# A gated attention and token-mixing block: first x block and wq loaded by columns, q ahead of k and v, and a PSUM bank of its own for the filler work

## The chip, the cores and the metric

The kernel runs on one NeuronCore of a Trainium2 chip. The metric is the device time of one execution in microseconds (us), lower is better. The engines are TensorE (PE, with its weight loads shown as PEld), VectorE (DVE), ScalarE (ACT), GpSimd (POOL) and SyncE (SP), which here issues all DMAs. Each engine works through its own instructions in order; semaphores tie the engines to one another.

## The reference

Two branches of the same input x (2048 tokens, 640 channels) are mixed by a gate of each token.

```python
def _A_ref(x, wq, wk, wv, wo):          # 32 heads of 20, one shared k and v
    q = (x @ wq) ...                     # (B, H, S, Dh)
    k = x @ wk
    v = x @ wv
    scores = jnp.einsum("bhqd,bkd->bhqk", q, k) * (Dh ** -0.5)
    o = jnp.einsum("bhqk,bkd->bhqd", _softmax(scores, axis=-1), v)
    return o.transpose(0, 2, 1, 3).reshape(B, S, H * Dh) @ wo

def _B_ref(x, w1, b1, w2, b2):          # token mixing, hidden size 1728
    h = _layernorm(x, axis=-1)
    u = _gelu(jnp.einsum("bsd,sf->bdf", h, w1) + b1)
    return (jnp.einsum("bdf,fs->bds", u, w2) + b2).transpose(0, 2, 1)

g = _sigmoid((x * gate_w).sum(-1, keepdims=True))
return g * _A_ref(x, ...) + (1 - g) * _B_ref(x, ...)
```

## The kernel before

Many operands are split into a high part (rounded to the matmul type fp32r) and a low part (the rest), and a product is made of three matmuls: high by high, high by low, low by high. A split is a cast (ACT or POOL) and a subtraction (DVE or POOL).

The work has three stages, and on each engine the order is the one in which the program writes it ("manual schedule").

**Stage 1: projections and layer norm** (lines 165 to 400), in four blocks `sb` of 512 tokens. Line 186 runs eight matmuls on a constant tile ahead of everything. `load_x(0)` (line 188) loads x block 0 as four tiles of 128 rows, each 640 floats wide, then come `wk`, `wv` and `gate_w` into `wkv` (lines 190 to 192), then the five row blocks of wq (lines 194 to 196; the first four lie in the buffers that x block 1 uses later), then the biases. At most eight DMAs of SP are outstanding: a ninth is issued when the first has landed. `transpose_x(0, range(DC))` (line 336, matmuls in line 272) turns all of block 0, 20 transposes into five PSUM banks, one for each column block `c`; `split_wkv` and `split_x` (lines 212 and 263) split `wkv` and the turned x; lines 340 to 344 split wq into `wq_hi` and `wq_lo`, three of the five subtractions on POOL and two on DVE (line 355).

Each block `sb` (loop in line 347) then runs: `pk`, ten matmuls that give k, v and the gate's logit; `split_kv`; `load_x(sb + 1)`; `store_k`; and for `m` in 0 to 4 the q projection of 128 columns, 15 matmuls (line 280), with `split_q` one step behind (a cast `qh` on ACT, a subtraction `ql` on DVE, two stores to `q_scr`). For m = 2, 3, 4 the next x block is transposed in between. `layer_norm(sb)` is a generator; each `next(norm)` gives DVE, POOL and ACT one more step: statistics in two steps, a power on POOL, then for each 128 rows the scaling `ht` (line 243), two casts on ACT and two subtractions on POOL. In block 0, `ahead` holds the high parts of q for m = 0 and 1, done in front of the loop. All projections share a PSUM pool of four banks (`psa`), the transposes another four (`pst`).

**Stage 2: the `pu` loop** (lines 519 to 557): for ten of the 14 column blocks of w1 the first mixing matmul of one half of the channels, 96 pairs of matmuls each into `pu` (line 540), 160 steps of six matmuls. In between, `lead()` runs two maximum matmuls `ms` (line 430), each followed by a DVE reduction (line 433): the row maxima of the scores that the softmax will subtract. 46 leads are spread over the steps and two follow behind the loop (line 556). `ms` rotates over three banks, `pu` over four. `gelu` works off its steps through `chain`.

**Stage 3: the main loop** (lines 909 to 966): attention in 512 rounds `k`. `beside` merges two lanes of 64 rows of the array: one with scores `s` (line 599) and maxima `ms`, one with "filler" matmuls `g` (the rest of the mixing block, then the output projection, lines 671, 783 and 834), and each round ends with the four `o` matmuls of the round before (line 626). `g` comes from pool `ps_g` (line 561), opened when the banks of `pu` have been given back, as are `ps_s` and `ps_o`.

Of the kernel before, what the change touches and what calls it, by code (L numbers as in the profile page):

```python
# [37 lines left out]
def mix_kernel(ctx: ExitStack, tc: tile.TileContext, A_x, A_wq, A_wk, A_wv, A_wo,  # L38
# [5 lines left out]
    def f32(ap):  # L44
        return ap.bitcast(F32)
# [118 lines left out]

    with tc.tile_pool(name="pa", bufs=1) as pa, \
            tc.tile_pool(name="pax", bufs=4) as pax, \
# [4 lines left out]
            tc.tile_pool(name="pst", bufs=4, space=PSUM) as pst, \  # L171
            tc.manual_schedule(engines=ALL):
        xts = {}

        def load(name, rows):
            t = pax.tile([P, D], F32, name=name)
            nc.sync.dma_start(out=t, in_=rows)  # L177
            return t

        def load_x(sb):  # L180
            for st in range(4 * sb, 4 * sb + 4):
                xts[st] = load(("xa", "xb")[sb % 2], x[st * P:(st + 1) * P, :])

        warm = psa.tile([P, NB], F32, name="pp")
        for i in range(8):
            nc.tensor.matmul(warm, kst[:, :P], kst[:, :NB], start=True, stop=True)

        load_x(0)
# [74 lines left out]
        def split_x(sb, c, pt):  # L263
            th, tl = x_tiles(sb, c)
            nc.scalar.activation(th, pt, AF.Copy)
            nc.vector.tensor_sub(tl, pt, f32(th))
# [68 lines left out]

        turned = transpose_x(0, range(DC))
        split_wkv()
        for t in turned:
            split_x(*t)
        for c in range(4):  # L340
            nc.gpsimd.tensor_copy(wq_hi[:, c, :], wqs[c])
        nc.scalar.activation(wq_hi[:, 4, :], wqs[4], AF.Copy)
        for c in range(3):
            nc.gpsimd.tensor_sub(wq_lo[:, c, :], wqs[c], f32(wq_hi[:, c, :]))

        due = None
        for sb in range(NQB):
            ts = [xT[sb, c] for c in range(DC)]
# [4 lines left out]
            if sb == 0:  # L353
                for c in range(3, DC):
                    nc.vector.tensor_sub(wq_lo[:, c, :], wqs[c], f32(wq_hi[:, c, :]))  # L355
            if sb + 1 < NQB:
                load_x(sb + 1)
            store_k(sb, k_hi, k_lo)
            norm = layer_norm(sb)
            next(norm)  # L360
            ahead = []
            if sb == 0:
                for m in range(2):
                    p = q_parts(m, ts)
                    ahead.append(project(p[0] + p[1], more=True))
            for m in range(DC):
# [28 lines left out]
                for _ in range(1 + (m > 1 or sb == 3)):  # L395
                    next(norm, None)
# [12 lines left out]
    ps_m = ctx.enter_context(tc.tile_pool(name="ps_m", bufs=3, space=PSUM))  # L409
    mpool = ctx.enter_context(tc.tile_pool(name="mpool", bufs=2))  # L410
# [103 lines left out]
    def pop_chain():  # L514
        f = chain.pop(0) if chain else None
        if f:
            f()

    with tc.tile_pool(name="psb", bufs=2, space=PSUM, side="right") as psb, tc.manual_schedule(engines=ALL):
# [8 lines left out]
        for fc in range(PRO):  # L528
            pu = [psb.tile([P, NB], F32, name=f"pu{r}") for r in range(2)]
            for hf in range(4):  # L530
# [4 lines left out]
                for c in range(HS):  # L535
# [6 lines left out]
                    done = [max(0, min(x, last) - skip) * (LEAD - 2) // (last - skip) for x in (at, at + 1)]  # L542
# [13 lines left out]
        for _ in range(2):  # L556
            lead()
# [3 lines left out]
    ps_g = ctx.enter_context(tc.tile_pool(name="ps_g", bufs=1, space=PSUM))  # L561
# [347 lines left out]
    with tc.manual_schedule(engines={mybir.EngineType.PE, mybir.EngineType.DVE, mybir.EngineType.Activation,  # L909
                                     mybir.EngineType.Pool, mybir.EngineType.SP}):  # L910
        def settle(k):
            for _ in range(2 if spare[0] else 1):
                f = later.pop(0) if later else None
                if f:
                    f()
            pop_chain()

        def visit(u):
            pv_mm(u)
            n, kb = units[u]  # L920
            if kb == 7 and n + 1 < NU:
                store_max(n + 1)
            if kb == 9 and n + 1 < NU:
                fetch_max(n + 1)

        for k in range(k_tail):
            b = k % 2
            ss = [lambda u=u, pr=pr: qk(u, pr, b) for u in (k - 1, k) for pr in range(2) if u >= 0]
            fs, rest, done = ph[k]
            ms = [[f for f in (ms_next(x) for _ in range(c)) if f] for x, c in (((b, 3), (1 - b, 1)) if len(fs) < 12 else ((b, 4), (1 - b, 0)))]  # L930
            lanes = [None, None]
            lanes[b] = lane_x(ss, ms[0])
            lanes[1 - b] = lane_f(ms[1], fs, done)
            beside(*lanes, b)
            ms_done()
            spare[0] = len(row_max) == NU
            settle(k)
            for f in rest:
                f()
            if k == k_tail - 4:  # L940
                raw = last_wo()
            if k == k_tail - 2:
                w_last = split_last(raw)
            if k:
                visit(k - 1)

        def stretch(k, n):
            lanes = [None, None]
            for b in range(2):
                own = [j for j in range(k, k + n) if j % 2 == b]  # L950
                ss = [lambda u=u, pr=pr, b=b: qk(u, pr, b) for j in own for u in (j - 1, j) for pr in range(2) if u < len(units)]
                fs = tail_take(b, math.ceil(len(tail[b]) * n / (len(units) + 1 - k)) + (n == 1) * (3 if not ss else -3))
                cut = [0] + [round(len(fs) * x) for x in ((0.25, 0.5, 0.75, 1.0) if n == 1 else
                                                              (0.18, 0.53, 0.82, 1.0) if b == k % 2 else (0.41, 0.71, 1.0, 1.0))]
                lanes[b] = [x for i in range(4) for x in [(X_US, y) for y in ss[i:i + 1]] +
                            [(F_US, f) for f in fs[cut[i]:cut[i + 1]]]]
            beside(*lanes, None)
            for j in range(k, k + n):
                settle(j)
                if 13 <= j - k_tail < 17:  # L960
                    tail_load(8 + j - k_tail - 13)
                visit(j - 1)

        stretch(k_tail, 1)
        for k in range(k_tail + 1, len(units), 2):
            stretch(k, 2)
        accs = {}

        for c in range(CUT // P, DC):
            r = min(P, HEAD - c * P)  # L970
            for st in held:
                oT, _ = room(8 + st - (NS - 4))
                for d in range(2):
                    if (st, d) not in accs:
                        accs[st, d] = (ps_g.tile([P, NB], F32, name="g") if (st, d) == (held[1], 1)
                                       else ps_m.tile([P, NB], F32, name="ms"))
                    for k, (j, w) in enumerate(((0, wo_hi), (1, wo_hi), (0, wo_lo))):
                        nc.tensor.matmul(accs[st, d][:, :HD2], oT[:r, j, c, :], w[:r, c, d * HD2:(d + 1) * HD2],
                                         start=(k == 0 and c == CUT // P), stop=False)
        assert not tail[0] and not tail[1]  # L980
        for f in later[1:]:
            f()
        oh, ol = osplit
        for i in range(4):
            st = NS - 4 + i
            for d in range(2):
                at = pp_pool.tile([P, NB], F32, name="p")
                sl = slice(d * HD2, (d + 1) * HD2)
                acc = accs.get((st, d)) or (ps_s.tile([P, NB], F32, name="s") if (i, d) != (3, 1)
                                            else ps_m.tile([P, NB], F32, name="ms"))  # L990
                for k, (o, w) in enumerate(((oh, w_last[0]), (ol, w_last[0]), (oh, w_last[1]))):
                    nc.tensor.matmul(acc[:, :HD2], o[:, i * P:(i + 1) * P], w[:, sl],
                                     start=(k == 0 and (st, d) not in accs), stop=(k == 2))
                if (i, d) in ((0, 0), (1, 0), (2, 1), (3, 0), (3, 1)):
# [27 lines left out]
```

## Time and profile before

| | us |
|---|---|
| median of 3 runs | 1707.94 (1707.88 to 1709.01) |
| the profiled execution, whole | 1709.46 |
| its span in the profile | 1707.7 |
| stage 1, until the first `pu` matmul | 100.2 |
| stage 2, until the last `pu` matmul ends | 185.3 |

A row of the timeline gives the start, the length, engine, line, operation, output and inputs with their shapes, and in brackets how long the engine stood idle before it and who released it. A group's row gives the count, the total busy time, the mean length in nanoseconds, and the idle time before its members. Lengths of matmuls overlap: the distance between starts says how fast PE goes. A row of windows gives the busy time of each engine in that stretch, in the order PE, PEld, DVE, ACT, POOL, then the clock granted to TensorE (1.00 is full), the share of the DMA engines and GB/s.

### The profile page before, as it was taken

What the parts mean: (1) busy time and instruction counts of PE and PEld (TensorE: products, weight loads), DVE (VectorE), ACT (ScalarE), POOL (GpSimd) and SP (SyncE); (2) the same over time, 40 slices, a digit from 0 to 9 for tenths busy, and PEclk for the clock granted to TensorE, in tenths of its full rate; (3) what the DMA queues carried; (4) which work ended last, traced back from release to release, by engine and by line L of the source; (5) the groups of instructions that cost most, each with busy time, mean ns of one, the idle gap of its engine ahead of it and who ended that gap; (6) DMA issues with size and microseconds to landing.
All of it is one profiled execution on the core that took longest, in us unless ns stands there. A gap on an engine that the chain in (4) does not pass through costs nothing.

```text
span 1707.7 us, 39022 instructions
## 1 busy us (share of the span) xinstructions
PE 1695.3 (99%) x14865; PEld 1103.4 (65%) x14865; DVE 1437.9 (84%) x2921; ACT 1188.1 (70%) x2316; POOL 567.5 (33%) x713
## 2 busy tenths in 40 slices
PE   9999999999999999999999999999999999999998
PEld 6899766666666666666666666666666666555666
DVE  6679889888889888888888888888888888888734
ACT  3444577777777777777777777777777777777775
POOL 5467545444444444322222222222221111111200
PEclk9999999999999999999999999999999999999999
DMA  6665322222222222121122222221111222345411
GB/s 201 197 169 141 99 62 63 63 70 76 55 74 64 70 64 74 50 56 53 48 70 70 67 62 62 61 57 53 57 46 42 62 62 64 85 119 145 130 57 57
DMA packets 170593, 135.45 MB, mean 79 GB/s; under 512 B 32633, under 2 KB 135446, under 8 KB 170406
## 3 DMA queue, kind: packets, MB, share of 16 engines
q1 hardware_dynamic: 170406, 132.96, 27.7%
q8 instruction: 117, 1.92, 0.5%
q14 instruction: 70, 0.57, 0.1%
HBM read 100.27 MB, written 31.65 MB: 77 GB/s over the span
## 4 chain that ended last, share of the span: by engine, by line
PE 96%; issue 2%; DVE 1%; DMA 1%; SPq 0%; ACT 0%; POOL 0%; POOLq 0%; ACTq 0%
PE o L626 30%; PE s L599 18%; PE ms L430 17%; PE g L671 12%; PE g L834 8%; PE pp L280 4%; PE pu L540 3%; PE g L783 2%; PE ms L740 1%; DVE mp L433 0%; SPq L177 0%; DMA ht<-in_A_wq_dram 0%; PE pt L272 0%; PE g L740 0%; DVE wq_lo L355 0%
## 5 line engine op out<-in xcount | busy, mean ns | idle before, releaser
L433 DVE TENSOR_REDUCE mp<-ms 128x1 f32<-128x512 f32 x2048 | 1278.1, 683 | 171.9 <-PE ms L430 169.9
L602 ACT ACTIVATE p<-s 128x512 f32<-128x512 f32 x2048 | 1069.0, 603 | 401.1 <-PE s L599 396.4
L430 PE MATMUL ms<-kst,qmx 60*128 60x512 f32 x2048 | 850.3, 422 | 3.4 <-DVE mp L433 2.9
L599 PE MATMUL s<-qst,kst 62*128 62x512 f32 x2048 | 746.2, 404 | 0.0
L626 PE MATMUL o<-p,v_sb 128*32 128x512 f32 x4096 | 554.7, 604 | 0.0
L430 PEld LDWEIGHTS ms<-kst,qmx 60*128 60x128 f32 x2048 | 379.7, 186 | 217.2 <-DVE flag L612 175.3
L599 PEld LDWEIGHTS s<-qst,kst 62*128 62x128 f32 x2048 | 378.6, 186 | 11.7 <-issue 10.9
L834 PE MATMUL g<-slot,wh 64*128 64x320 f32 x1152 | 282.4, 319 | 0.0
L124 POOL TENSOR_TENSOR wl<-wr,wh 128x512 fp32r<-128x512 f32 (+1 forms) x176 | 220.4, 1254 | 36.3 <-ACT wh L121 22.3
L834 PEld LDWEIGHTS g<-slot,wh 64*128 64x128 f32 x1152 | 191.2, 185 | 59.9 <-DVE flag L612 59.9
L123 POOL CAST wh<-wr 128x512 fp32r<-128x512 f32 (+1 forms) x136 | 79.8, 587 | 444.9 <-PE g L671 282.1
L671 PE MATMUL g<-slot,wh 64*128 64x320 f32 x864 | 209.0, 317 | 0.0
L671 PE MATMUL g<-u,wh 64*128 64x320 f32 x864 | 208.9, 317 | 0.0
L626 PEld LDWEIGHTS o<-p,v_sb 128*32 128x32 f32 x4096 | 93.3, 108 | 138.8 <-issue 131.5
L834 PE MATMUL g<-slot,wl 64*128 64x320 f32 x576 | 179.9, 312 | 0.0
L671 PEld LDWEIGHTS g<-slot,wh 64*128 64x128 f32 x864 | 142.4, 184 | 40.2 <-DVE flag L612 39.4
L671 PEld LDWEIGHTS g<-u,wh 64*128 64x128 f32 x864 | 142.2, 184 | 40.2 <-DVE flag L612 40.2
L671 PE MATMUL g<-slot,wl 64*128 64x320 f32 x432 | 135.0, 313 | 0.0
L671 PE MATMUL g<-u,wl 64*128 64x320 f32 x432 | 134.7, 312 | 0.0
L834 PEld LDWEIGHTS g<-slot,wl 64*128 64x128 f32 x576 | 106.5, 185 | 15.1 <-DVE flag L612 15.1
L671 PEld LDWEIGHTS g<-slot,wl 64*128 64x128 f32 x432 | 79.6, 184 | 13.4 <-DVE flag L612 13.4
L671 PEld LDWEIGHTS g<-u,wl 64*128 64x128 f32 x432 | 79.4, 184 | 13.4 <-DVE flag L612 13.4
(184 smaller groups left out, 1412.3 us busy)
## 6 DMA issues: line engine op xcount, KB each, us to landing
wr<-in_B_w_dram SPq DMA_DIRECT2D x152, 256.0 KB
qmx<-q_scr SPq DMA_DIRECT2D x192, 80.0 KB
qst<-q_scr SPq DMA_DIRECT2D x192, 80.0 KB
q_scr<-qh SPq DMA_DIRECT2D x20, 256.0 KB
q_scr<-ql SPq DMA_DIRECT2D x20, 256.0 KB
y_scr<-yo SPq DMA_DIRECT2D x16, 320.0 KB
slot<-o_scr SPq DMA_DIRECT2D x16, 320.0 KB
o_scr<-oh SPq DMA_DIRECT2D x124, 40.0 KB
```

The costliest lines, as they stand in the source:

```text
L123: nc.gpsimd.tensor_copy(wh, wr)
L124: nc.gpsimd.tensor_sub(wl, wr, f32(wh))
L280: nc.tensor.matmul(pp, w, t, start=first and n == 0, stop=not more and n == len(steps) - 1)
L430: nc.tensor.matmul(ms, qmax[n][64 * b:64 * b + 60, pr, qt * P:(qt + 1) * P], kst[64 * b:64 * b + 60, kq * NB:(kq + 1) * NB], start=True, s ...
L433: nc.vector.tensor_reduce(mtiles[n][:, c, kq:kq + 1], ms, axis=AX.X, op=ALU.max)
L540: nc.tensor.matmul(pu[r][:, :HD2], w[rows, c, :], h[rows, st, :], start=(st == 0 and k == 0), stop=(st == NS - 1 and k == 2))
L599: nc.tensor.matmul(s, kst[64 * b:64 * b + 62, kb * P:(kb + 1) * P], q[64 * b:64 * b + 62, pr, :], start=True, stop=True)
L602: nc.scalar.activation(p, s, AF.Exp, scale=SCALE)
L626: nc.tensor.matmul(o[32 * hh:32 * hh + 32, :], v_sb[:, kb, :], ptiles.pop((u, hh)), start=(kb == 0), stop=(kb == NS - 1), skip_group_check ...
L671: other_tile(half, nc.tensor.matmul(hold["p"][:, :HD2], w[r, fc % HS, :], u[d][r, fc, :], start=(hold["n"] == 1), stop=(hold["n"] == 6 * F ...
L783: other_tile(half, nc.tensor.matmul(hold["p"][:, :HD2], o[r, c, :], w[r, c, d * HD2:(d + 1) * HD2], start=(hold["n"] == 1), stop=(hold["n" ...
L834: other_tile(half, nc.tensor.matmul(hold["p"][:, :HD2], w[r, st % HS, :], h[d][r, st, :], start=(hold["n"] == 1), stop=(hold["n"] == 6 * NS)))
```

## The change

In block 0 of stage 1:

- x block 0 lies in one tile `xin[0]` and is loaded in five column blocks of 128 (rows of 512 bytes), each followed by the first 384 columns of the wq rows that it meets. The remaining 256 columns of wq (`wqs2`) go into three of the buffers that w1 uses later, behind `wkv`.
- Six constant matmuls in place of eight.
- `first_block` takes the column blocks one by one: cast of wq on POOL, four transposes, split of x, and six q matmuls (three `m`, high and low part of x); the transposes of block c + 1 stand ahead of the q matmuls of block c on PE. So `ahead` holds three `m`, and `pk` comes after them.
- `load_x(1)` is issued there, `split_wkv` moves from DVE to ACT and POOL, all low parts of wq are made on POOL, the casts of its last 256 columns on ACT, and three steps of `layer_norm(0)` stand in front of `pk`; later m steps take one step each in block 0.

In stages 2 and 3: `ps_g` is opened ahead of the `pu` loop and keeps its bank; all 48 leads lie in the steps of the loop; round 0 of the main loop gives its first two maxima three slots each. The manual schedule covers everything from stage 1 on in one scope; lines 909 to 1000 only lose an indent.

```diff
+    ctx.enter_context(tc.manual_schedule(engines=ALL))
...
+        xin = [pa.tile([P, 4, D], F32, name=name) for name in ("xa", "xb")]
+        xts = {st: xin[st // 4 % 2][:, st % 4, :] for st in range(NS)}
+        QW = 3 * P
...
-        for i in range(8):
+        for i in range(6):
             nc.tensor.matmul(warm, kst[:, :P], kst[:, :NB], start=True, stop=True)
-        load_x(0)
+        wqs = [(xin[1][:, c, :] if c < 4 else tmp.tile([P, D], F32, name="ht"))[:, :QW] for c in range(DC)]
+        more = [w1r.tile([P, HS, P], F32, name="wr").rearrange("p (i j) f -> p i (j f)", i=2) for _ in range(3)]
+        wqs2 = [more[c // 2][:, c % 2, :] for c in range(DC)]
+        for c in range(DC):
+            nc.sync.dma_start(out=xin[0][:, :, c * P:(c + 1) * P],
+                              in_=x[:NB, c * P:(c + 1) * P].rearrange("(t p) d -> p t d", p=P))
+            nc.sync.dma_start(out=wqs[c], in_=A_wq[c * P:(c + 1) * P, :QW])
...
-        wqs = [load("xb", A_wq[c * P:(c + 1) * P, :]) for c in range(4)]
-        wqs.append(tmp.tile([P, D], F32, name="ht"))
-        nc.sync.dma_start(out=wqs[4], in_=A_wq[4 * P:, :])
+        for c in range(DC):
+            nc.sync.dma_start(out=wqs2[c], in_=A_wq[c * P:(c + 1) * P, QW:])
...
-                nc.vector.tensor_copy(hi, wkv[:, :, j, :DH + j])
-                nc.vector.tensor_sub(lo, wkv[:, :, j, :DH + j], f32(hi))
+                nc.scalar.activation(hi, wkv[:, :, j, :DH + j], AF.Copy)
+                nc.gpsimd.tensor_sub(lo, wkv[:, :, j, :DH + j], f32(hi))
...
+        def wq_low(c, cols, raw):
+            nc.gpsimd.tensor_sub(wq_lo[:, c, cols], raw, f32(wq_hi[:, c, cols]))
+        def first_q(c, j, ahead):
+            for m, pp in enumerate(ahead):
+                nc.tensor.matmul(pp, wq_hi[:, c, m * P:(m + 1) * P], xT[0, c][j], start=c == 0 and j == 0, stop=False)
+        def first_block():
+            ahead = [psa.tile([P, NB], F32, name="pp") for _ in range(QW // P)]
+            def turn(c):
+                nc.gpsimd.tensor_copy(wq_hi[:, c, :QW], wqs[c])
+                split_x(*transpose_x(0, (c,))[0])
+            turn(0)
+            for c in range(DC):
+                if c + 1 < DC:
+                    turn(c + 1)
+                for j in range(2):
+                    first_q(c, j, ahead)
+                wq_low(c, slice(0, QW), wqs[c])
+            load_x(1)
+            split_wkv()
+            for c in range(DC):
+                nc.scalar.activation(wq_hi[:, c, QW:], wqs2[c], AF.Copy)
+            for c in (0, 3, 1, 4, 2):
+                wq_low(c, slice(QW, D), wqs2[c])
+            norm = layer_norm(0)
+            for _ in range(3):
+                next(norm)
+            return ahead, norm
...
         for sb in range(NQB):
+            ahead, norm = first_block() if sb == 0 else ([], layer_norm(sb))
...
-            if sb == 0:
-                for m in range(2):
-                    p = q_parts(m, ts)
-                    ahead.append(project(p[0] + p[1], more=True))
...
-                for _ in range(1 + (m > 1 or sb == 3)):
+                for _ in range(1 + (sb and m > 1 or sb == 3)):
                     next(norm, None)
...
     ps_m = ctx.enter_context(tc.tile_pool(name="ps_m", bufs=3, space=PSUM))
+    ps_g = ctx.enter_context(tc.tile_pool(name="ps_g", bufs=1, space=PSUM))
...
-                    done = [max(0, min(x, last) - skip) * (LEAD - 2) // (last - skip) for x in (at, at + 1)]
+                    done = [max(0, min(x, last) - skip) * LEAD // (last - skip) for x in (at, at + 1)]
...
-        for _ in range(2):
-            lead()
...
-    ps_g = ctx.enter_context(tc.tile_pool(name="ps_g", bufs=1, space=PSUM))
...
+        if k == 0:
+            (m0, m1, m2), (s0, s1) = ms[0], ss
+            lanes[0] = [(3 * X_US, m0), (3 * X_US, m1), (X_US, s0), (X_US, m2), (X_US, s1)]
```

More of the change, by code (lines that the diff above doesn't have):

```diff
@@ L352, in mix_kernel @@
             kv, k_hi, k_lo = split_kv(pk)
-            if sb == 0:
-                for c in range(3, DC):
-                    nc.vector.tensor_sub(wq_lo[:, c, :], wqs[c], f32(wq_hi[:, c, :]))
-            if sb + 1 < NQB:
+            if 0 < sb < NQB - 1:
                 load_x(sb + 1)
             store_k(sb, k_hi, k_lo)
[L359 to L362, printed above, removed]
-                for m in range(2):
-                    p = q_parts(m, ts)
-                    ahead.append(project(p[0] + p[1], more=True))
+            if sb:
+                next(norm)
             for m in range(DC):
@@ L517, in pop_chain @@
             f()
[L519 removed]
+    with tc.tile_pool(name="psb", bufs=2, space=PSUM, side="right") as psb:
         at, skip, last = 0, 5, NS * PRO - 6
@@ L908, in mix_kernel @@
     w1_upto(4 * PRO + 4)
[L909 to L938, printed above, removed]
-                f()
[L940 to L981, printed above, removed]
-            f()
-        oh, ol = osplit
-        for i in range(4):
-            st = NS - 4 + i
-            for d in range(2):
[L987 to L994, printed above, removed]
-                    nc.vector.scalar_tensor_tensor(at[:, :HD2], acc[:, :HD2], g_col[:, st:st + 1], parts[st][:, sl],
-                                                   op0=ALU.mult, op1=ALU.add)
-                else:
-                    nc.scalar.activation(at[:, :HD2], acc[:, :HD2], AF.Copy, scale=g_col[:, st:st + 1])
-                    nc.gpsimd.tensor_add(at[:, :HD2], at[:, :HD2], parts[st][:, sl])
-                nc.sync.dma_start(out=y_out[st * P:(st + 1) * P, sl], in_=at[:, :HD2])
@@ new lines, in mix_kernel @@
+    stretch(k_tail, 1)
+    for k in range(k_tail + 1, len(units), 2):
+        stretch(k, 2)
+    accs = {}
+    for c in range(CUT // P, DC):
+        r = min(P, HEAD - c * P)
+        for st in held:
+            oT, _ = room(8 + st - (NS - 4))
+            for d in range(2):
+                if (st, d) not in accs:
+                    accs[st, d] = (ps_g.tile([P, NB], F32, name="g") if (st, d) == (held[1], 1)
+                                   else ps_m.tile([P, NB], F32, name="ms"))
+                for k, (j, w) in enumerate(((0, wo_hi), (1, wo_hi), (0, wo_lo))):
+                    nc.tensor.matmul(accs[st, d][:, :HD2], oT[:r, j, c, :], w[:r, c, d * HD2:(d + 1) * HD2],
+                                     start=(k == 0 and c == CUT // P), stop=False)
```

88 lines of the change are left out of this document (70 added, 18 removed).

## The prediction

> **What bounds the kernel now.** I read the page first, for the engine that sets the end.
>
> ```profile
> span 1707.7 us, 39022 instructions
> ...
> PE 1695.3 (99%) x14865; PEld 1103.4 (65%) x14865; DVE 1437.9 (84%) x2921; ACT 1188.1 (70%) x2316; POOL 567.5 (33%) x713
> ```
>
> TensorE (PE) is busy 99% of the span, so only time in which it stands still or runs slowly can be gained. PE's timeline, and the chain of waits in order of time at the seam between the `pu` loop and the main loop, show where that is.
>
> ```profile
> 1.43 3.61 PE L186 MATMUL pp<-kst 128*128 128x512 f32 x8 [1.43 <-DVE kst L63]
> 4.88 0.60 PE L272 MATMUL pt<-ident,xa 128*128 128x128 f32 x4
> ...
> 7.55 0.65 PE L272 MATMUL pt<-ident,xa 128*128 128x128 f32 x4
> 8.04 0.27 PE L272 MATMUL pp<-ident,xa 128*128 128x128 f32 x1
> 9.07 2.80 PE L280 MATMUL pp<-slot,wkv_s 128*128 128x512 f32 x8 [0.76 <-ACT slot L265]
> ...
> 21.86 0.82 PE L272 MATMUL pt<-ident,xb 128*128 128x128 f32 x6
> ...
> 34.85 2.04 PE L280 MATMUL pp<-slot,wkv_s 128*128 128x512 f32 x8
> 36.73 0.40 PE L280 MATMUL pp<-xT_hi,wkv_s 128*128 128x512 f32 x1
> 36.96 0.39 PE L280 MATMUL pp<-xT_lo,wkv_s 128*128 128x512 f32 x1
> ```
>
> ```profile
> 182.65 2.62 PE pu L540 x34
> ...
> 185.91 0.49 DVE yo L476
> 186.40 1.21 DVE mp L433 x2
> ```
>
> Two places. **The start:** the first projection begins at 9.07, after all of x block 0 is loaded, transposed and split; block 1's first projection ends at 36.96 + 0.39 = 37.35. That point is my mark, since PE stands nowhere between it and the `pu` loop. **The seam:** PE's last `pu` matmul ends at 185.27. The last gelu's add on DVE waits for ACT, the four row-maximum reductions of the last two `lead()` calls stand behind it, and PE needs their banks.
>
> ```profile
> 186.00:187.00 1.00, 0.00 (x0) 0.00 (x0) 1.00 (x3) 0.47 (x1) 0.92 (x2) 1.00 0.83 226
> 189.00:193.00 4.00, 4.00 (x26) 3.16 (x26) 3.84 (x8) 2.01 (x5) 1.77 (x3) 0.57 0.64 180
> ```
>
> ```profile
> 192.97 1.07 PE L626 MATMUL o<-p,v_sb 128*32 128x512 f32 x8
> ```
>
> In the windows (length, then busy time of PE, PEld, DVE, ACT and POOL, granted clock, DMA share, GB/s) PE is idle for the whole microsecond from 186, and from 189 to 193 its clock averages 0.57. DVE is busy almost without a break. The first `o` matmuls come at 192.97, 7.70 us after the `pu` loop's end.
>
> **The change, part by part: the start.** I walk five queues of the changed kernel's instruction order, with these prices.
>
> ```profile
> L266 DVE TENSOR_TENSOR slot<-pt,slot 128x512 fp32r<-128x512 f32 x8 | 5.0, 680 | 0.0
> L225 DVE BATCH_NORM_STATS2 st<-xa 128x6 f32<-128x320 f32 x8 | 3.4, 468 | 0.0
> L293 DVE TENSOR_TENSOR ql<-pp,qh 128x512 fp32r<-128x512 f32 x4 | 2.7, 676 | 3.2 <-ACT qh L292 3.2
> L243 DVE TENSOR_SCALAR ht<-xa,mv,rstd 128x640 f32<-128x640 f32 x4 | 2.3, 606 | 0.0
> ```
>
> ```profile
> L247 ACT ACTIVATE slot<-ht 128x320 fp32r<-128x320 f32 x8 | 3.1, 460 | 4.7 <-DVE ht L243 4.7
> L292 ACT ACTIVATE qh<-pp 128x512 fp32r<-128x512 f32 x4 | 2.4, 588 | 5.0 <-PE pp L280 5.0
> ```
>
> ```profile
> L344 POOL TENSOR_TENSOR wq_lo<-xb,wq_hi 128x640 fp32r<-128x640 f32 x3 | 5.2, 1769 | 0.0
> L341 POOL CAST wq_hi<-xb 128x640 fp32r<-128x640 f32 x4 | 2.9, 721 | 7.0 <-DMA xb<-in_A_wq_dram 6.7
> ...
> L234 POOL TENSOR_TENSOR r<-ve,mhalf 128x4 f32<-128x4 f32 x1 | 1.0, 1049 | 3.8 <-DVE ve L233 3.8
> ```
>
> ```profile
> 2.00:6.60 4.60, 4.13 (x18) 3.19 (x16) 0.00 (x0) 0.00 (x0) 1.75 (x6) 1.00 0.95 287
> 6.60:8.40 1.80, 1.53 (x10) 1.05 (x10) 0.49 (x3) 0.49 (x1) 0.00 (x0) 1.00 0.65 94
> 46.00:47.00 1.00, 1.00 (x6) 0.84 (x5) 0.65 (x2) 1.00 (x2) 0.46 (x1) 1.00 1.13 338
> ```
>
> *DMA.* x in column blocks has rows of 512 bytes. w1's loads, of the same shape, run at 338 GB/s around 46 us, so the short rows cost nothing against 287 GB/s for x now. Block c of x is 262 KB, the first 384 columns of a wq row block 197 KB: at 0.29 MB/us a pair takes 1.55 us. Bytes flow from about 2.1 us, and x's 1.31 MB, through at about 6.6, had landed at 7.55 (PE waits until then), so landing lags by up to 0.95. x block 0 lands by 3.95, block c 1.5c later, the fifth at about 10, its wq half a microsecond behind.
>
> *PE.* Eight warm-up matmuls take 4.88 − 1.43 = 3.45, so six end at 4.02. Then per c four transposes (0.11 each) and six matmuls (0.234 each: 36.96 − 34.85 over nine): 1.85, longer than 1.55, so PE sets the pace: transposes of c=1 at 5.5, last q matmul issued at 14.2. POOL keeps up: 3/5 of 0.72 per cast and of 1.77 per subtraction make 1.49 per c; its last cast ends at about 11, its last subtraction at 13.1, the two small `wkv` subtractions (no row: above 0, below one 0.72 us cast each; 0.4 taken) at 14. The k/v projection, ten matmuls, runs 14.2 to 16.7. Moving the `wkv` split from DVE to ACT and POOL costs nothing as long as q runs until 14.2; with q done sooner, up to the 0.9 taken would lie on PE's path.
>
> *Late next.* Low parts for m=0 and 1, 2.3 us, and the v transposes reach 19.4. Then come the transposes of x block 1, whose DMA now stands on SP behind ten loads, three `wkv` loads, five second-half wq loads and four bias loads, at most eight of them outstanding by the built order's waits. Bytes: 2.29 MB until 10.0, `wkv` 1.8 us (the 94 GB/s window), 0.66 MB in 2.2, lag 0.95: SP issues x block 1 at about 15; 1.31 MB at 0.29 and the lag end at 20.5. So PE waits 1.1 there. From those transposes to block 1's first projection PE took 34.85 − 21.86 = 12.99 before; ten matmuls of m=2 (2.34) are now done earlier: 10.65, hence 31.15, and 33.65 at the mark, ten matmuls later.
>
> *A second chain ends at the same time.* The statistics (3.4 us, and five small instructions at 0.2, which is above 0 and below the 0.6 of ht) go in front of the k/v evacuation and end at 17.2, hidden behind the projection. POOL's five subtractions of 256 columns (0.71 each) and the power (1.05) end at 18.7, and DVE waits for the power with everything queued behind it: all q low parts and the splits of x block 1. After four more small ones for `rstd`, each m alternates between DVE and ACT: ht 0.57, two casts 0.78, qh 0.60, ql 0.67 = 2.6. Four of them, and five splits of 0.62: 19.5 + 10.4 + 3.1 = 33.0 for the last low part of block 1, which the mark's last matmul needs: 33.4. I take 33.85, for the hand-overs between engines that both sums leave out. **Gain 37.35 − 33.85 = 3.5**, bounded by 4.8 (x block 1 there at 19.4 and the second chain hidden: 32.55) and by 0.5 (rival D).
>
> **The seam.** Two leads move into the loop (48 instead of 46 over 149 steps), `g` has a bank that no `pu` tile had, and round 0 spaces its first two maxima. After the `pu` end DVE has the add until +1.08, then reductions of 0.605 each; round 1's last maximum needs the fifth to be done, +4.1, so `o` starts at +4.4 against +7.70: 3.3 gained. The four moved matmuls cost PE up to 0.6 in the loop (0.15 each, half a full-height matmul, as two rows of tiles run beside each other). DVE was busy there for
>
> ```profile
> 100.20:185.30 85.10, 83.33 (x1055) 81.48 (x1055) 73.50 (x123) 38.67 (x74) 61.81 (x54) 1.00 0.57 155
> ```
>
> 73.5 of 85.1; 2.4 more leaves 9 free, so I charge 0.3 for late reductions. **Gain 2.4**, bounds 0 and 3.3. The extra bank costs nothing (3 + 1 + 4 = 8); with a shared bank the first filler would wait until +1.08. The scope of the hand-written order moves only a few weight splits on ACT and POOL; after round 0 PE's order is the old one, so the 1500 us behind it shift as they are.
>
> Sum: 1707.7 − 3.5 − 2.4 = **1701.8** span, 1703.6 for that execution (1709.46 with what lies around). The median of the runs is 1707.94, so **1702.0**.
>
> The Trainium skill, "TensorE: Matmul & The Clock Gate", Part 1, has the clock fall to half only after an idle window of about 3.4 us. The windows above show a fall after PE's stop of under 2 us; the measurement decides, and my sum lets the half clock go with the gap. By the rule the gap would not be its cause; what that gives is rival A.
>
> **Rivals.**
>
> *A, the half clock stays.* The gap goes and the clock still falls after the seam. Lost from 189 to 193: 4 × (1 − 0.57) = 1.7, so 1703.7. For: behind the seam PE waits for DVE's reductions in any case. Against: the stalls in the `pu` loop (rival C) left its clock at 1.00 in the row above. This is the skill's rule above as a mechanism.
>
> *B, a cold start.* The grouped weight loads of the warm-up and of the first transposes (count, busy us, mean ns):
>
> ```profile
> L186 PEld LDWEIGHTS pp<-kst 128*128 128x128 f32 x6 | 2.0, 330 | 0.6
> ```
>
> ```profile
> L272 PEld LDWEIGHTS pt<-ident,xa 128*128 128x128 f32 x15 | 1.7, 141 | 1.2 <-DMA xa<-in_A_x_dram 1.1
> ```
>
> They sped up from 330 to 141 ns at about 4.6, after 3.2 us of unbroken work. Now the matmuls end at 4.02 and PE stands from 4.5 to 5.5. If the clock stays low for two stretches of 3.4 us, q loses 3.4, of which 1.1 was waiting for x block 1: +2.4, 1704.4. Against: x block 0 lies ready by 3.95, so the work is unbroken until 4.5.
>
> *C, slower.* DVE becomes the bound of the `pu` loop: PE runs in order, so a late reduction stops the `pu` matmuls behind it. Waits before:
>
> ```profile
> PE ms L430 <- DVE mp L433: 2.9, 3, 1.5
> ```
>
> The longest is the seam's, so two lie in the loop, 1.4 us together. Were each of its ten blocks to cost the longest, 1.5, that is 15 less 1.4 = 13.6 more, so 1715.6; from 5.9 us of new waits on, 0.6 a block, the change loses. Against: 9 us of DVE are free.
>
> *D, the change doesn't do what it says.* The ten loads share the same engines; if they land bunched near 10 rather than in turn, q starts at 8 to 10 and the mark moves by 3: 1705.0. Against: PE transposes the first x rows at 4.88, 2.7 us before the fourth's.
>
> **How the numbers follow.** Forecast 0.52, a better case without either late chain (4.8 + 2.4: 1700.7) 0.05, A 0.13, B 0.13, C 0.08, D 0.09. The range, 1699.2 to 1705.2, holds the forecast with its bounds (4.8 + 3.3 gained would be 1699.8), A, B and most of D. A difference of 0.2% is 3.4 us, about what can be told from no change: faster means under 1704.5, which takes in the forecast, the better case, A and some of B: 0.78; within it half of B, D: 0.14; slower: 0.08.
>
> **What would show it.** Block 1's projection ends at 33 to 34.5; first q matmul at 5.5 to 6; PE waits for x block 1 at 19 to 20; weight loads of the first q matmuls at 188 ns and not 330; `o` starts 4 to 5 us after the `pu` end, at a clock of 1.00; waits of `ms` on `mp` in the `pu` loop under 2.5 us. I am wrong if PE waits anew in the main loop, if q's matmuls come at the warm-up's 0.43, or if DVE's chain reaches past 35.

## The result, and the profile after

| | before | after |
|---|---|---|
| median of 22 runs each, us | 1708.46 | 1706.23 |
| lowest to highest | 1707.03 to 1709.93 | 1703.37 to 1707.40 |
| span of the profiled execution | 1707.7 | 1704.5 |

The ratio is 0.9984, 95% interval 0.9978 to 0.9991: about 2.2 us gained, where 5.9 were forecast, and just outside the range (1699.2 to 1705.2). The mechanism at the seam came as forecast. The start gained nothing and cost a little.

First PE's timeline of the changed kernel at its very start (start, length, engine, line, operation, operands; in brackets the idle time ahead and who ended it).

```profile
4.16 1.05 PE L273 MATMUL pt<-ident,xa 128*128 128x128 f32 x4
6.19 1.11 PE L273 MATMUL pt<-ident,xa 128*128 128x128 f32 x4 [0.97 <-DMA xa<-in_A_x_dram]
6.95 2.77 PE L342 MATMUL pp<-slot,wq_hi 128*128 128x512 f32 x6
9.56 0.60 PE L273 MATMUL pt<-ident,xa 128*128 128x128 f32 x4
```

The second column block of x landed at 6.19 (forecast 5.45), and the first six q matmuls took 2.61 from start to start, which is 0.43 each instead of 0.23. Next the same view around the mark, with the transposes of v of block 1 (line 318) as the first landmark behind it, and the start of the `pu` loop.

```profile
32.25 2.12 PE L281 MATMUL pp<-slot,wkv_s 128*128 128x512 f32 x8
35.78 0.50 PE L281 MATMUL pp<-xT_hi,wkv_s 128*128 128x512 f32 x1 [1.42 <-ACT xT_hi L266]
36.62 0.71 PE L281 MATMUL pp<-xT_lo,wkv_s 128*128 128x512 f32 x1 [0.33 <-DVE xT_lo L267]
37.12 1.91 PE L281 MATMUL pp<-slot,wq_hi 128*128 128x512 f32 x4
...
42.09 0.42 PE L318 MATMUL pt<-ident,kv 21*128 21x21 f32 x4
```

```profile
101.46 0.56 PE L557 MATMUL pu<-slot,wh 64*128 64x320 f32 x4
```

PE reached block 1's first projection at 32.25, and then stood 1.42 and 0.33 us for the split of the last column of x. The mark is 36.62 + 0.71 = 37.33, against 37.35 before. Behind it four matmuls take 1.91 where the same four took 1.09, and the transposes of v come at 42.09 against 40.77: **the start ends 1.3 us later than before**. One execution stands against one here: in the four seam experiments below that have the start of before, the first `pu` comes at 99.21 to 100.53, so the loss is 0.9 to 2.3, by which one is taken. These windows of the changed kernel say why (length, busy time of PE, PEld, DVE, ACT, POOL, then the granted clock, DMA share, GB/s).

```profile
34.40:36.60 2.20, 0.50 (x1) 0.19 (x1) 1.32 (x3) 1.82 (x5) 1.68 (x2) 1.00 0.23 86
36.80:40.00 3.20, 3.20 (x8) 2.52 (x9) 2.28 (x6) 1.22 (x2) 0.47 (x1) 0.50 1.10 237
```

A stop, then 3.2 us at half clock. What PE waited for stands in the chain of waits of the changed kernel (start, length, what): it begins with the evacuation of the first projection and the transposes of v, and from 23.0 on it is a ping-pong between DVE and ACT.

```profile
18.99 0.60 ACT kv L300
...
20.35 0.44 PE pt L318 x4
...
21.19 1.15 DVE r L237
...
22.96 0.63 DVE ht L244
23.61 0.83 ACT slot L248 x2
24.47 0.61 ACT qh L293
25.10 0.69 DVE ql L294
...
35.88 0.69 DVE xT_lo L267
```

Then the seam, from the timeline of the changed kernel: the `pu` loop ends at 185.76 + 0.31 = 186.07 and the first `o` comes 4.53 later, against 7.61 before (measured alike, from the last `pu` row's end). The granted clock is 1.00 throughout.

```profile
185.76 0.31 PE L557 MATMUL pu<-slot,wl 64*128 64x320 f32 x1
190.60 1.06 PE L640 MATMUL o<-p,v_sb 128*32 128x512 f32 x8
```

So the 3.2 us between the two spans are: start +1.3 (first `pu` at 101.46 against 100.12), `pu` loop −0.6 (84.61 against 85.24), seam −3.1, and −0.8 in the 1514 us behind. The medians differ by 2.2 only, since the profiled execution of the kernel before took 1709.46, 1.0 above its median. The seam's difference is far outside what equal code shows from one execution to the next, the start's just outside; the −0.6 and the −0.8 are inside. The ten profiled kernels with the new loop took 83.8 to 85.1 in it, the three with the old one 84.4 to 85.2, and the stretch behind took 1513.7 to 1514.9 in all of them.

### The profile page after: what moved, and what is told of

It reads as the page before. It is cut to its first block, busy times and chain, and to the rows that moved or that the text cites. A ratio compares the mean times of both kernels' runs of the same rounds, so it can differ in the third digit from the quotient of the medians.

```text
span 1704.5 us, 39051 instructions
## 1 busy us (share of the span) xinstructions
PE 1693.6 (99%) x14863; PEld 1105.1 (65%) x14863; DVE 1433.5 (84%) x2915; ACT 1189.2 (70%) x2322; POOL 571.0 (34%) x723
## 3 DMA queue, kind: packets, MB, share of 16 engines
q8 instruction: 117, 1.92, 0.5%
## 4 chain that ended last, share of the span: by engine, by line
PE 94%; issue 2%; DVE 2%; DMA 1%; ACT 1%; POOL 0%; SPq 0%; POOLq 0%; DVEq 0%; ACTq 0%
PE o L640 30%; PE s L613 18%; PE ms L447 17%; PE g L685 12%; PE g L848 8%; PE pu L557 3%; PE pp L281 3%; PE g L797 2%; PE ms L754 1%; PE pp L342 0%; DVE mp L450 0%; PE pt L273 0%; ACT slot L248 0%; DMA xa<-in_A_x_dram 0%; PE g L754 0%
## 5 line engine op out<-in xcount | busy, mean ns | idle before, releaser
L685 PEld LDWEIGHTS g<-slot,wh 64*128 64x128 f32 x864 | 142.3, 184 | 40.2 <-DVE flag L626 40.2
```

The source lines that it names most:

```text
L685: other_tile(half, nc.tensor.matmul(hold["p"][:, :HD2], w[r, fc % HS, :], u[d][r, fc, :], start=(hold["n"] == 1), stop=(hold["n"] == 6 * F ...
```

## Experiments

The kernel before ran again beside each group of experiments, with medians of 1708.06 to 1708.46. A difference between two changed kernels is one of medians from different groups, and 0.4 us of it can come from that.

### The two parts alone

The kernel before with the seam's part (the edit is the last five hunks of the diff: `ps_g`, `LEAD`, the two trailing leads, the spacing), and the changed kernel with the seam of before.

> The kernel before with the seam's part alone: a bank of its own for g, all 48 leads in the pu loop, round 0 spaced. Theory (the seam's step of the prediction was right, the start gave the gain back): first o 4.4 to 4.6 us after the pu loop's end (before 7.70), clock 1.00 throughout, 2.4 to 3.4 us less than before. Rival (the gap at the seam is only moved, into late reductions in the pu loop): pu loop 1 to 3 us longer and less than 1 us gained.

> The changed kernel with the seam of before, so the start's part alone. Theory (the start gained nothing because its second chain began 3.4 us late, and the stop that it makes costs half a clock): mark at 37.3 as before, clock 0.5 to 0.7 from 36 to 40, the transposes of v of block 1 1.3 us later than before, 0.5 to 1.3 us more than before in all. The prediction's step: mark 33.85 and 3.5 us less. Rival (the start did gain, and something behind the seam lost it): 2 us less or better.

Seam alone: 1704.42, ratio 0.998 (0.9971 to 0.999), 3.6 us gained. Start alone: 1710.9 against 1708.06, ratio 1.0013 (1.0004 to 1.0022), 2 to 3 us **lost**. Timelines of the seam alone, then of the start alone:

```profile
184.29 0.31 PE L541 MATMUL pu<-slot,wl 64*128 64x320 f32 x1
188.65 1.06 PE L624 MATMUL o<-p,v_sb 128*32 128x512 f32 x8
```

```profile
6.52 1.11 PE L273 MATMUL pt<-ident,xa 128*128 128x128 f32 x4 [1.30 <-DMA xa<-in_A_x_dram]
...
37.32 0.50 PE L281 MATMUL pp<-xT_lo,wkv_s 128*128 128x512 f32 x1 [0.34 <-DVE xT_lo L267]
37.66 1.68 PE L281 MATMUL pp<-slot,wq_hi 128*128 128x512 f32 x4
...
42.78 0.42 PE L318 MATMUL pt<-ident,kv 21*128 21x21 f32 x4
```

At the seam `o` comes 4.05 after the end (4.36 from the start of the last `pu`, the way the expectation for the spacing counts). The start alone loses more than was expected: in its profile x's second block landed another 0.3 later (6.52), everything behind shifts, and the transposes of v stand at 42.78, 2.0 later than before. Its loss is not the same in each run: nine of eleven took 1710.3 to 1711.6, two 1708.1 and 1708.2. Nor do the parts add up (+2.8 and −3.6 against −2.2 for both); why is open. The rival that something behind the seam had eaten the start's gain falls.

### The second chain: order on DVE and ACT

In m = 1 to 3 of block 0, DVE had `ql` (which waits for ACT's `qh`) ahead of `ht`, and ACT had the casts of `ht` ahead of the next `qh`: each engine waited for the other in turn. The edit puts `ht` ahead of the q split and its casts behind.

```diff
                 nc.vector.tensor_scalar(ht, blk[i], mv[:, i, 0:1], rstd[:, i:i + 1],
                                         op0=ALU.subtract, op1=ALU.mult)
+                if sb == 0:
+                    yield
                 for d in range(2):
...
                 if m:
+                    if sb == 0:
+                        next(norm, None)
                     split_q(*due)
...
-                for _ in range(1 + (sb and m > 1 or sb == 3)):
+                for _ in range(1 + (sb and m > 1 or sb == 3 or sb == m == 0)):
                     next(norm, None)
```

> The changed kernel with ht of block 0 put in front of the q split on DVE, its casts behind that split on ACT, for m = 1 to 3; nothing else. Theory (the alternation ht, casts, qh, ql between DVE and ACT sets the mark): each m takes 2.5 us or less on DVE, PE does not stop ahead of xT_hi and xT_lo of block 1, mark at 34.6, no half clock behind it, the transposes of v of block 1 at about 38.1, 4.0 us less than the changed kernel, about 6 less than before. Rival (the cold first q matmuls set the mark): unchanged within 0.6 us, mark at 36.5 or later.

1702.81, ratio 0.9969 (0.9956 to 0.9981): 3.4 us less than the changed kernel (3.0 if each is taken against the kernel before of its own group). PE's timeline of this kernel, and its window:

```profile
32.28 2.03 PE L283 MATMUL pp<-slot,wkv_s 128*128 128x512 f32 x8
...
34.39 0.39 PE L283 MATMUL pp<-xT_lo,wkv_s 128*128 128x512 f32 x1
34.62 1.09 PE L283 MATMUL pp<-slot,wq_hi 128*128 128x512 f32 x4
...
38.19 0.42 PE L320 MATMUL pt<-ident,kv 21*128 21x21 f32 x4
```

```profile
36.80:40.00 3.20, 3.20 (x17) 2.40 (x16) 2.67 (x11) 0.65 (x2) 1.29 (x1) 1.00 0.90 279
```

PE arrives at the same 32.28, finds the low part ready (DVE makes it at 32.15), and goes on: mark 34.78, transposes of v at 38.19, 17 matmuls instead of 8 in the same 3.2 us. Nothing of the start's first 22 us was touched: the first `ht` begins at 22.99, as late as in the changed kernel, but from there to the last low part it is 9.8 us instead of 13.6. With that, 2.6 of the 3.5 us that were forecast at the mark are there. So it is shown that the second chain took the start's gain, and the rival that the cold q matmuls set the mark falls. Why a chain in the old order came late, though the forecast had it end in time, is told below.

### The stop and the clock

The changed kernel, with matmuls whose result nobody reads put where PE stood. The chain and the mark stay.

```diff
+                pk = project(steps[:8], more=True)
+                idle = pst.tile([P, NB], F32, name="pt")
+                for i in range(6):
+                    nc.tensor.matmul(idle, wq_hi[:, 0, :P], ts[0][0], start=True, stop=True)
+                nc.tensor.matmul(pk, *steps[8], start=False, stop=False)
```

(and two more ahead of `steps[9]`)

> The changed kernel with six idle matmuls (operands that lie ready, a result that nobody reads) ahead of the ninth matmul of block 1's first projection and two ahead of the tenth: the second chain and so the mark stay where they are, but PE does not stand. Theory (the stop brings the half clock): mark at 37.3 to 37.6, clock 1.00 from 36 to 42, the transposes of v of block 1 at 40.8 to 41.1 instead of 42.09, 1.0 to 1.4 us less than the changed kernel. Rival (the half clock comes from something else in the stretch): clock 0.5 as before, nothing gained.

1704.47, ratio 0.9974 (0.9964 to 0.9984), 1.8 us less than the changed kernel. PE's timeline of this kernel:

```profile
37.00 0.50 PE L382 MATMUL pp<-xT_lo,wkv_s 128*128 128x512 f32 x1
37.34 1.09 PE L281 MATMUL pp<-slot,wq_hi 128*128 128x512 f32 x4
...
40.91 0.42 PE L318 MATMUL pt<-ident,kv 21*128 21x21 f32 x4
```

The mark is at 37.5 (37.33 in the changed kernel), but the four matmuls behind it take 1.09 and the transposes of v come at 40.91. PE's stop cost its length and then another 1.2 us of half clock; eight idle matmuls buy the second part back.

### The cold first q matmuls

Ten warm-up matmuls for six, in the changed kernel and with `ht` ahead.

```diff
-        for i in range(6):
+        for i in range(10):
             nc.tensor.matmul(warm, kst[:, :P], kst[:, :NB], start=True, stop=True)
```

> The changed kernel with ten warm-up matmuls in place of six, nothing else. Theory (cold q matmuls only delay the second chain): first q matmuls at 0.23 us each instead of 0.43, k and v projection ends at 16.4 to 17.0 instead of 18.95, DVE's first ht at 20.5 to 21.5 instead of 22.96, mark at 35 to 35.6, PE still stops there for about as long as before the edit and the half clock follows; 1.5 to 2.5 us less than the changed kernel. Rival (the cold start is all that failed): mark at 33.9, no stop, 3.5 to 5 us less than the changed kernel. Rival (a stop of PE at about 6 us lets the first q matmuls be slow however long the warm-up): q still at 0.43 and nothing gained.

> ht put in front of the q split, and ten warm-up matmuls in place of six. Theory (with the alternation gone PE alone sets the mark, so the 1.0 us of cold q matmuls comes on top): no stop, mark at 33.7 to 33.9, transposes of v of block 1 at 37.2, 4.4 us less than the changed kernel, 1.0 less than with ht ahead alone. Rival (the second chain is still the bound, only later seen): PE stops again ahead of the mark, mark at 34.5 or later, nothing gained over ht ahead alone.

1705.74 (0.9984, 0.9975 to 0.9992) and 1702.08 (0.9961, 0.9949 to 0.9974). Timeline of the changed kernel with ten:

```profile
7.14 1.63 PE L342 MATMUL pp<-slot,wq_hi 128*128 128x512 f32 x6 [0.25 <-ACT slot L266]
...
34.81 0.50 PE L281 MATMUL pp<-xT_hi,wkv_s 128*128 128x512 f32 x1 [1.41 <-ACT xT_hi L266]
...
41.10 0.42 PE L318 MATMUL pt<-ident,kv 21*128 21x21 f32 x4
```

With ten, the q matmuls are warm (1.63 for six), every later landmark is 1.0 earlier, and the stop of 1.41 stays as long as it was, with the half clock behind it. I had expected 1.5 to 2.5 us, because I counted all of the 2.25 us by which the first projection was late as cold clock; ten warm-ups win back 1.0 of it. With `ht` ahead there is no stop, and the mark comes at 33.84. In the time the gain is 0.5 with the stop, inside the spread of the runs, so that only the traces show it. Without the stop it is 0.7 (1.0 against the kernel before of each group), and no run of the one kernel reaches into those of the other (1701.2 to 1702.2 and 1702.6 to 1703.0).

### DVE's first step of the chain

> The changed kernel with POOL's subtraction k_lo of block 0 (1.27 us) and the stores of k behind the first m step, nothing else. Theory (DVE's first r, 128 x 4 elements, took 1.22 us because POOL's k_lo ran in the same stretch, and with it the whole second chain came 1.0 us late): r at 0.15 to 0.2 us, first ht at 21.8 to 22.0 instead of 22.96, mark at 36.1 to 36.5, PE's stop 0.5 to 0.9 us instead of 1.75; 1.0 us less than the changed kernel if the half clock stays, 2.3 less if it goes with the shorter stop. Rival (r was long for another reason): r still above 1 us, nothing gained.

DVE's `r` in the changed kernel and, in the second fence, in this one; in the third, POOL in the changed kernel:

```profile
21.11 1.22 DVE L237 TENSOR_TENSOR r<-r 128x4 f32<-128x4 f32 x1
```

```profile
19.85 0.15 DVE L237 TENSOR_TENSOR r<-r 128x4 f32<-128x4 f32 x1
...
20.64 0.61 DVE L244 TENSOR_SCALAR ht<-xa,mv,rstd 128x640 f32<-128x640 f32 x1
...
31.90 0.69 DVE L294 TENSOR_TENSOR ql<-pp,qh 128x512 fp32r<-128x512 f32 x1 [4.13 <-DMA q_scr<-ql]
```

```profile
21.03 1.27 POOL L305 TENSOR_TENSOR k_lo<-kv,k_hi 20x512 fp32r<-20x512 f32 x1 [0.50 <-ACT k_hi L304]
```

The step is as expected: away from POOL's subtraction, `r` takes 0.15. That `ht` comes 2.3 earlier, and not 1.0, has a second reason, in PE's timeline of this kernel:

```profile
6.57 1.92 PE L343 MATMUL pp<-slot,wq_hi 128*128 128x512 f32 x6
```

With the same six warm-ups x's second block landed at 5.80 and the first six q matmuls took 1.92, so the first projection ended 1.25 earlier. What the cold start costs differs from execution to execution. The time (1705.88) says nothing on its worth, because my edit brought a wait of its own: the stores of k now stood on SP in front of the q stores, and the third `ql` waited 4.13 us for a buffer. What the 1.1 us alone are worth was not measured.

### The parts of the seam

Each takes one thing out of the seam's part alone: the spacing of round 0, the two leads moved into the loop, the bank of `g`.

> The seam's part alone, without the spacing of round 0's first maxima (bank of its own and 48 leads in the loop stay). Theory (the leads behind the loop were the cost, the spacing only spares a short wait): first o 4.6 to 5.2 us after the pu loop's end instead of 4.36, 0.2 to 0.8 us of the gain of 3.6 lost. Rival (the spacing carries the gain): first o later than 6 us after the end, less than 1.5 us gained against before.

> The seam's part alone, but 46 leads in the loop and two behind it as before (bank of its own and spacing stay). Theory (the four reductions behind the last add are the cost): PE stops again for about 1.4 us, half clock some 2 us behind the stop, first o 6.8 to 7.7 us after the end, 1 us or less gained against before. Rival (the shared bank of g was the cost): first o at 4.4 to 5, the gain stays.

> The seam's part alone, but g's bank opened behind the loop as before, in a bank that a pu tile had (48 leads in the loop and spacing stay). Theory (the first filler waits for the last add, 1.1 us): first o 5.0 to 5.6 us after the end, 2.4 to 3.0 us gained against before, no half clock. Rival (the bank costs nothing, since PE has maxima and scores to do meanwhile): 4.4, and 3.3 to 3.7 gained.

| | median us | ratio to before | `o` after the loop's end | PE's stop |
|---|---|---|---|---|
| seam's part whole | 1704.42 | 0.998 (0.9971 to 0.999) | 4.05 | none |
| without the spacing | 1705.61 | 0.9987 (0.9978 to 0.9996) | 5.19 | 0.96 |
| leads behind the loop | 1707.66 | 0.9994 (0.9985 to 1.0003) | 7.68 | 1.44 |
| bank of `g` shared | 1707.04 | 0.9994 (0.9986 to 1.0003) | 5.50 | 1.29 |

Timeline and window with the leads behind the loop, then the timelines without the spacing and with the shared bank:

```profile
185.48 1.10 PE L431 MATMUL ms<-kst,qmx 60*128 60x512 f32 x2 [1.44 <-DVE mp L434]
```

```profile
187.60:190.60 3.00, 3.00 (x16) 2.95 (x17) 2.88 (x7) 1.76 (x3) 1.58 (x3) 0.50 0.68 198
```

```profile
184.88 0.47 PE L597 MATMUL s<-qst,kst 62*128 62x512 f32 x1 [0.96 <-PE g L832]
```

```profile
185.65 0.53 PE L832 MATMUL g<-slot,wh 64*128 64x320 f32 x2 [1.29 <-POOL wh L123]
```

The leads are the largest piece, as argued: with them behind the loop the old stop and the half clock are back. But the other two are not small. The spacing is worth 1.2 where I expected 0.2 to 0.8, and the bank 2.6 where I expected about 1: a shared bank holds the first filler for 1.3 us, and PE, which runs in order, has nothing to do behind it. POOL's cast is named as the releaser only because it came last: in the seam's part whole the filler begins 0.8 us ahead of that cast. DVE's add, which frees the bank, ends at 185.51 in that trace. Of the 2.6, the later `o` shows 1.45; where the rest comes from is open. The pieces sum to more than the whole, since any one of them left out makes a stop.

### A version that beats both

`ht` ahead, six warm-ups, then the transposes of c = 0, three more constant matmuls, the high-part q matmuls of c = 0, and only then the transposes of c = 1. In a second kernel the first lead of the `pu` loop moves from step 5 to step 8.

```diff
             turn(0)
+            for i in range(3):
+                nc.tensor.matmul(warm, kst[:, :P], kst[:, :NB], start=True, stop=True)
+            first_q(0, 0, ahead)
...
-                for j in range(2):
+                for j in range(c == 0, 2):
                     first_q(c, j, ahead)
...
-        at, skip, last = 0, 5, NS * PRO - 6
+        at, skip, last = 0, 8, NS * PRO - 6
```

> ht put in front of the q split; six warm-up matmuls, then the transposes of c = 0, three more constant matmuls, the three q matmuls of c = 0's high part, and only then the transposes of c = 1. Theory (PE has no stop until 7, so it is warm, and the first q matmuls need not wait for the second column block): first q matmul at 5.8 to 6.0, 0.23 us each, last q matmul issued at 15.0 to 15.3, mark at 33.2 to 33.6; 1.2 to 1.6 us less than with ht ahead alone. Rival (the next column blocks land later than PE could take them): PE waits for x or POOL's casts at c = 2 or 3, mark as with ten warm-ups or later.

> Both parts, ht ahead of the q split, the filled start (six warm-ups, three constant matmuls, first q ahead of the second column block), and the first lead of the pu loop at step 8 instead of 5. Theory (PE's only stop between 5 us and the seam is ms behind the last ql of stage 1, 1.1 us at about 101): that wait falls to 0.2 or less, 0.7 to 1.1 us less than with the first lead at step 5, 1699.8 to 1700.2. Rival (the wait comes back as late reductions, as the same 48 leads lie in fewer steps): within 0.3 us of that kernel.

1700.84 (0.9956, 0.9943 to 0.9968) and 1700.36 (0.9952, 0.9938 to 0.9966): 7.5 and 7.9 us less than the kernel before in the same comparisons. Timeline of the first of them:

```profile
4.86 1.63 PE L355 MATMUL pp<-kst 128*128 128x512 f32 x3
6.29 1.14 PE L344 MATMUL pp<-slot,wq_hi 128*128 128x512 f32 x3
...
15.27 2.03 PE L283 MATMUL pp<-slot,wkv_s 128*128 128x512 f32 x8
...
33.18 0.39 PE L283 MATMUL pp<-xT_lo,wkv_s 128*128 128x512 f32 x1
```

The mark is 33.57, as expected, though the first q matmuls come at 6.29 and not at 5.9, and three of them still take 1.14. The first kernel gains 2.0 on `ht` ahead alone, a little over the 1.2 to 1.6 expected; the mark and the first `pu` come 1.2 earlier. The later first lead takes away the wait of 1.1 us that PE had for the last `ql` at the start of the `pu` loop (its waits in the loop are 0.9 on `mp` in all), but the medians differ by 0.5, and the spans are 1699.3 and 1699.0: whether it gains anything isn't settled.

## Why the prediction was wrong

**The step that failed** is "A second chain ends at the same time": its beginning, not its length. Forecast were 19.5 for the first `ht` and 13.5 us from there to the last low part. Measured were 22.96 and 13.6 (to 36.57). The 3.46 us are the whole of the missing 3.5 at the mark:

- 2.25 from the first projection, which ended at 18.95 instead of 16.7. Of it 0.7 is x's second block, landed at 6.19 instead of 5.45: I had taken 0.29 MB/us from the first bytes on, and the trace has 231 GB/s between 4 and 6. The other 1.5 is the cold start of rival B: the transposes of c = 1 took 0.76 to the next start where 0.44 was charged, and the six q matmuls behind them 2.61 where 1.40 was. Ten warm-ups win back only 1.0, because they end 1.6 later themselves. The prediction has the cold q matmuls as rival B, but prices them on PE's path alone and not on this chain.
- 1.1 from `r`, a 128 x 4 multiplication charged with 0.2, that took 1.22.
- 0.1 to 0.2 because the wait was another one. The prediction has DVE wait for POOL's power until 18.7. The power ended at 20.53, but `r` stood on DVE behind the copies of v, which waited for v's transposes, and began at 21.11:

```profile
19.49 1.04 POOL L235 TENSOR_TENSOR r<-ve,mhalf 128x4 f32<-128x4 f32 x1 [0.53 <-DVE ve L234]
```

Both signs that the prediction names for being wrong at the start came: q's matmuls at 0.43, and DVE's chain past 35.

**What the sum left out** is the price of a stop. The second chain had been put level with PE's own (33.4 and 33.65). PE's own came at 34.78 where nothing was in its way, 1.1 late; but the second came at 37.33, so PE stood 1.75 us, and a stop is not paid by its length alone: the half clock behind it took 1.2 to 1.4 more. That this follows a short stop stood in the prediction for the seam, and was not carried over to the start, where a stop of 1.1 was forecast at its length alone. So the start's term was +1.3 instead of −3.5.

**The other steps.** x in short rows lands in turn (rival D falls); that short rows cost nothing is not shown, since the loads ran at 231 to 243 GB/s between 2 and 6 us and nothing separates the rows from the order of the loads. PE took 1.83 per column block, as forecast (1.85). It did not wait for x block 1: the forecast 1.1 there was wrong, in the good direction. Moving the `wkv` split and the low parts of wq to ACT and POOL cost nothing: the power on POOL waited for DVE's statistics (19.24), not for the subtractions, which ended at 18.97. Rival B had the right mechanism and too high a price (2.4, where its own sum, 3.4 less 1.1, gives 2.3; the rows show 1.5). Rival A did not come at the seam, rival C not at all: PE waits 0.9 us on `mp` in the loop, below the 2.5 given.

**The seam** was right in mechanism (`o` at +4.53, forecast +4.4) and too small in the sum: the 0.9 charged for moved matmuls and late reductions was not paid. The loop did not get longer, 84.61 against 85.24, with four more maxima in it; the difference itself lies inside the spread given above. PE's waits in it are nearly the same in sum, 1.6 against 1.7: less for `mp` (0.9 against 1.4 in the loop), but a new one for the last `ql` of stage 1. The waits of PE in the changed kernel's loop and seam (us in total, times, longest):

```profile
PE ms L447 <- DVE mp L450: 0.9, 2, 0.6
PE ms L447 <- DVE ql L294: 0.7, 1, 0.7
```

Seam alone gained 3.6 where 2.4 was forecast.

## What to carry to other kernels

When a stage is pulled forward, follow the slowest hand-over between the helper engines from its first link: work that hid behind the old wait is now the wait. Two engines that split their jobs in the same loop should each issue first what the other waits for; here an exchange of two instructions was worth 3.0 to 3.4 us, and the change itself 2.2. A stop of PE costs its length and may cost more behind it (1.2 to 1.4 us here), so keep it busy with anything, and give back the banks it needs next.

## What the runs showed of the hardware

**The half clock comes in pieces of 3.4 us, and a stop of under 2 us can be enough.** In the changed kernel the clock falls at about 36.8 and returns at about 40.2. It fell there behind stops of 1.42 + 0.33 us, and likewise behind one of 1.44 with the leads behind the loop (187.4 to 190.8) and one of 1.45 in the kernel before (189.0 to 192.4). It did not fall behind stops of 0.96 and 1.29, nor behind one of 1.46 in the kernel with the late `k_lo` (its next stop, 1.41 + 0.33, did it). The Trainium skill, "TensorE: Matmul & The Clock Gate", Part 1, has a free-running window of that length, and the lengths agree; but it asks for an idle window, and these runs fall with about half of one.

**The rows of the granted clock do not show a cold start.** Window and grouped weight loads (count, busy us, mean ns) of the changed kernel, then the loads with ten warm-ups:

```profile
6.00:8.00 2.00, 1.81 (x7) 1.62 (x8) 0.61 (x2) 0.60 (x1) 0.98 (x2) 1.00 1.04 317
```

```profile
L342 PEld LDWEIGHTS pp<-slot,wq_hi 128*128 128x128 f32 x6 | 1.9, 332 | 0.4
```

```profile
L342 PEld LDWEIGHTS pp<-slot,wq_hi 128*128 128x128 f32 x10 | 1.7, 188 | 0.8 <-issue 0.5
```

The clock stands at 1.00 while the matmuls take 0.43 and the loads 332 ns. For the first microseconds the lengths of the matmuls have to be read.

**A small DVE operation can take as long as POOL's beside it.** `r`, with two inputs from SBUF, took 1.22 to 1.24 in block 0 of each kernel in which POOL's `k_lo` began just before it, and 0.15 there in the kernel before and with the late `k_lo`, where it did not. In blocks 2 and 3 it took 1.16 and 1.24 in the kernel before too: there it ran beside POOL's `wl` subtraction of 128x512 (70.14 to 71.43 and 90.00 to 91.29) and ended with it, at 71.46 and 91.31. The Trainium skill, "GPSIMD Engine Reference", Specifications, has the two engines share their SBUF interface, with contention for DVE instructions that have two SBUF inputs; the runs agree.
